# Linear-attention numerator: one reciprocal per sign, the division by the common denominator on GpSimd, and a longer lag of the output projection

## The chip, the cores and the metric

The kernel runs on one core of a Trainium2 chip. The metric is device microseconds (us) of one execution; a time given for a kernel is the median of several. In the profile the engines are PE (TensorE, matmuls), PEld (its weight loads), DVE (VectorE), ACT (ScalarE), POOL (GpSimd) and SP (SyncE, which here issues nearly all DMAs). A difference of about 0.5% is the least that a measurement of this kernel can tell from no change.

## The reference, cut to what matters

Two branches, A (linear attention) and B (an expert that runs for one token), are mixed by a gate per token. Only A is touched here.

```python
def _A_ref(x, wqkv, w_phi, wo):                       # S = 2048, D = 1024, H = 32 heads, Dh = 32
    q, k, v = split(x @ wqkv)
    pq, pk = per_head(q, w_phi), per_head(k, w_phi)
    phi_q = concat([softmax(pq), softmax(-pq)])       # two signs, 32 features each
    phi_k = concat([softmax(pk), softmax(-pk)])
    kv = einsum("bhsf,bhsd->bhfd", phi_k, v)
    z  = einsum("bhsf->bhf", phi_k)
    num = einsum("bhqf,bhfd->bhqd", phi_q, kv)
    den = einsum("bhqf,bhf->bhq", phi_q, z) + 1e-6
    return (num / den) @ wo

g = sigmoid((x * gate_w).sum(-1))
out = g * A + (1 - g) * B                             # B = x, plus one row from the expert
```

Written per head and token, with E+ = exp(pq) and E- = exp(-pq): sign s has a softmax sum S_s, a raw numerator N_s = E_s @ kv_s and a raw denominator D_s = E_s @ z_s. The wanted value is (N+/S+ + N-/S-) / (D+/S+ + D-/S-).

## The kernel before, in words

A first part makes x transposed (`xT`), the v projection, the folded weights `wkf` and `wqf` (w_phi multiplied into wk and wq) and the gates. A second part walks over keys and sums kv and z in PSUM. `kv_finish` (L431 to L452) copies them into `KV`. The third part, the one changed here, goes over queries; in the profile its first unit starts at 173.04 us.

- `q_front(sb, j)` (L458 to L467): for a block of 512 tokens and 128 features, 8 matmuls `pq` (L464) and two exps on ACT into `E` (L466, L467). There are 32 calls.
- `q_num(t, hf)` (L469 to L504): a *unit*. 32 units = 16 tiles `t` of 128 tokens x two halves `hf` of the heads. 8 matmuls `num` (L485), 4 per sign; each gives 128 numerator columns and 8 more (128 to 135) with each head's denominator and softmax sum. Then on DVE: `ds` (L489), `pr` (L491), `den` (L493), `rden` (L495), two halves of `ab` (L497, L498), and the large product `T` (L500, 128x1024 out of PSUM). GpSimd adds the two signs of `T` into `o_sb` (L504).
- `q_oT(t)` (L506 to L520): when both halves of a tile are there, a DMA transpose `oT` (L512) issued by SP; for the last tile 8 PE transposes into PSUM (`oT_ps`, L516) and a copy on ACT (L517). ACT also makes `xg`, the tile's share of x (L519).
- `q_wo(t, nh)` (L522 to L532): half an output tile: 8 matmuls `po` (L528), the gate and the addition of `xg` on DVE (`o_out`, L530), the store by SP (L532).

`num` has one buffer (three PSUM banks; pool `psK`, `bufs=1`): the matmuls of a unit wait until `T` of the unit before has read it. `po` and `oT_ps` share a ring of two PSUM banks (pool `psB`), handed out in the order of the code.

The loop at L596 to L612 sets the order: in step i unit n = i - 4, the transpose of the unit before it, front i, and one waiting `q_wo`. Units come in groups of eight (first halves of four tiles, then their second halves), so tiles become whole in units 4 to 7 of each group. A tile's two `q_wo` join the queue with a due step:

```python
wq_ += [(i + WL - 1, t, 0), (i + WL - 1, t, 1)]      # L605, WL = 4
```

In every other step, as long as there are any, 32 narrow matmuls of the expert (L374) come in as well. On every engine the instructions stand in a fixed order, made when the program is built from this loop and from what is ready when; the matmuls of one call can be split around those of another.

Of the kernel before, what the change touches and what calls it, by code (L numbers as in the profile page):

```python
# [8 lines left out]
BF = mybir.dt.bfloat16  # L9
F32 = mybir.dt.float32  # L10
I32 = mybir.dt.int32
U32 = mybir.dt.uint32
ALU = mybir.AluOpType
ACTF = mybir.ActivationFunctionType
AX = mybir.AxisListType
# [3 lines left out]
P = 128  # L19
S = 2048  # L20
D = 1024
H = 32
DH = 32
NT = S // P
KB = D // P
FF = 3584
NFB = FF // P
HH = 16
# [7 lines left out]
RANGE2 = 900.0  # L36
VC = [0, 352, 704, 1026]
VW = 1026


def general_path(tc, A_wqkv, A_w_phi, A_wo, x2, out2, gate, omg, y2, idx_pool, xT, wqf, ident, BDm):
# [116 lines left out]
def _bc(ap, shape):  # L158
    return ap.unsqueeze(len(shape) - 1).to_broadcast(shape)
# [3 lines left out]
def kernel(  # L163
# [4 lines left out]
    nc = tc.nc  # L168
# [10 lines left out]
    sm = main.enter_context(tc.tile_pool(name="sm", bufs=4))  # L179
# [34 lines left out]
    gate = const.tile([P, NT], F32, name="gate")  # L214
# [28 lines left out]
    def xload(t):  # L243
        xt_ = xs.tile([P, D], BF, name="xs_t", tag="xs")
        nc.sync.dma_start(out=xt_[:], in_=x2[t * P:(t + 1) * P, :])
        xtiles[t] = xt_

    wv_sb = wraw.tile([P, KB, VW], BF, name="wv_sb", tag="w16")
    xload(0)
# [6 lines left out]
    def rows_in():  # L256
        rows_ps = m2_ps[:, 0:KB].bitcast(BF)
        nc.tensor.transpose(out=rows_ps, in_=rows[:], identity=ident[0:2 * KB, 0:2 * KB])
        nc.vector.tensor_copy(out=wv_sb[:, :, D:VW].rearrange("p k c -> p c k"),
                              in_=rows_ps.rearrange("p (c k) -> p c k", c=2))  # L260
# [127 lines left out]
    def k_v(t, c):  # L388
# [7 lines left out]
        if c == 2:  # L396
            nc.vector.tensor_copy(out=rg[:, :, t], in_=pv[:, D - lo:VW - lo])

# [33 lines left out]
    def kv_finish():  # L432
        kvr = kvps[:, 0:16 * KSTR].rearrange("p (j half c) -> p j half c", half=2, c=KSTR)
        n = 0
        for half in range(2):
            for hh_ in range(2):
                h4 = half * 2 + hh_
                dst = slice(h4 * 32, h4 * 32 + 32)
                for sg in range(2):
                    q = hh_ * 2 + sg  # L440
                    src = slice(q * 32, q * 32 + 32)
                    zc = (128 + h4) if sg == 0 else (132 + h4)
                    sc = (132 + h4) if sg == 0 else (128 + h4)
                    kv_src = kvr[src, :, half, hh_ * 33:hh_ * 33 + DH]
                    z_src = kvr[src, :, half, hh_ * 33 + DH:hh_ * 33 + DH + 1]
                    if n % 2 == 0:
                        nc.vector.tensor_copy(out=KV[dst, sg, :, h4 * 32:h4 * 32 + 32], in_=kv_src)
                    else:
                        nc.scalar.copy(out=KV[dst, sg, :, h4 * 32:h4 * 32 + 32], in_=kv_src)
                    nc.vector.tensor_scalar_add(out=KV[dst, sg, :, zc:zc + 1], in0=z_src, scalar1=1e-6)  # L450
                    nc.gpsimd.memset(KV[dst, sg, :, sc:sc + 1], 1.0)
                    n += 1  # L452
# [16 lines left out]
    def q_num(t, hf):  # L469
        qw = qp["qw"]  # L470
        sb, tl = divmod(t, 4)
        E = est[sb]
        if hf == 0:
            st = {"o": qw.tile([P, H, DH], BF, name="o_sb", tag="o_sb", bufs=5)}
            xin = qw.tile([P, D], BF, name="xin", tag="xin", bufs=6)
            nc.sync.dma_start(out=xin[:], in_=x2[t * P:(t + 1) * P, :])
            st["xin"] = xin
            ost[t] = st
        st = ost[t]
        num = psK.tile([P, 3 * 512], F32, name="num", tag="kvn")  # L480
        for sg in range(2):
            for jl in range(4):
                b = sg * 4 + jl
                j = hf * 4 + jl
                nc.tensor.matmul(num[:, b * NSTR:b * NSTR + KVW], lhsT=E[:, j, sg, tl * P:(tl + 1) * P],  # L485
                                 rhs=KV[:, sg, j, :], start=True, stop=True)
        nb = num[:, 0:8 * NSTR].rearrange("p (b c) -> p b c", c=NSTR)
        ds = sm.tile([P, 4, 8], F32, name="ds", tag="ds")
        nc.vector.tensor_copy(out=ds[:], in_=nb[:, 4:8, 128:136])  # L489
        pr = sm.tile([P, 4, 8], F32, name="pr", tag="pr")  # L490
        nc.vector.tensor_tensor(out=pr[:], in0=nb[:, 0:4, 128:136], in1=ds[:], op=ALU.mult)  # L491
        den = sm.tile([P, 4, 4], F32, name="den", tag="den")
        nc.vector.tensor_tensor(out=den[:], in0=pr[:, :, 0:4], in1=pr[:, :, 4:8], op=ALU.add)  # L493
        rden = sm.tile([P, 4, 4], F32, name="rden", tag="rden")
        nc.vector.reciprocal(out=rden[:], in_=den[:])  # L495
        ab = sm.tile([P, 2, 4, 4], F32, name="ab", tag="ab")
        nc.vector.tensor_tensor(out=ab[:, 0, :, :], in0=nb[:, 4:8, 128:132], in1=rden[:], op=ALU.mult)  # L497
        nc.vector.tensor_tensor(out=ab[:, 1, :, :], in0=nb[:, 0:4, 132:136], in1=rden[:], op=ALU.mult)  # L498
        T = qw.tile([P, 2, HH, DH], F32, name="T", tag="T", bufs=2)
        nc.vector.tensor_tensor(  # L500
            out=T[:].rearrange("p s (j h) d -> p (s j) h d", h=4),
            in0=nb[:, :, 0:128].rearrange("p b (h d) -> p b h d", d=DH),
            in1=ab[:].rearrange("p s j h -> p (s j) h").unsqueeze(3).to_broadcast([P, 8, 4, DH]), op=ALU.mult)
        nc.gpsimd.tensor_tensor(out=st["o"][:, hf * HH:(hf + 1) * HH, :], in0=T[:, 0], in1=T[:, 1], op=ALU.add)  # L504

    def q_oT(t):  # L506
        qw = qp["qw"]
        st = ost[t]
        o_f = st["o"][:].rearrange("p h d -> p (h d)")
        oT = qw.tile([P, KB, P], BF, name="oT", tag="oT", bufs=3)  # L510
        if t < NT - 1:
            nc.sync.dma_start_transpose(out=oT[:], in_=o_f)  # L512
        else:
            oT_ps = psB.tile([P, KB, P], BF, name="oT_ps", tag="pB")
            for kb in range(KB):
                nc.tensor.transpose(out=oT_ps[:, kb, :], in_=o_f[:, kb * P:(kb + 1) * P], identity=ident[:])  # L516
            nc.scalar.copy(out=oT[:], in_=oT_ps[:])  # L517
        xg = qw.tile([P, D], F32, name="xg", tag="xg", bufs=2)
        nc.scalar.activation(out=xg[:], in_=st["xin"][:], func=ACTF.Copy, scale=omg[:, t:t + 1])  # L519
        st["oT"], st["xg"] = oT, xg  # L520

    def q_wo(t, nh):  # L522
        qw = qp["qw"]
        st = ost[t]
        sl = slice(nh * 512, (nh + 1) * 512)
        po = psB.tile([P, 512], F32, name="po", tag="pB")
        for kb in range(KB):
            nc.tensor.matmul(po[:], lhsT=st["oT"][:, kb, :], rhs=wo_sb[:, kb, sl], start=(kb == 0), stop=(kb == KB - 1))  # L528
        o_out = qw.tile([P, 512], BF, name="o_out", tag="o_out", bufs=4)
        nc.vector.scalar_tensor_tensor(out=o_out[:], in0=po[:], scalar=gate[:, t:t + 1],  # L530
                                       in1=st["xg"][:, sl], op0=ALU.mult, op1=ALU.add)
        nc.sync.dma_start(out=out2[t * P:(t + 1) * P, sl], in_=o_out[:])  # L532

    wq = [(0, kb) for kb in range(KB)] + [(1, kb) for kb in range(KB)]
# [38 lines left out]
    for i in range(NU + LAG):  # L573
# [9 lines left out]
        if i == 28:  # L583
            range_flag()
    qp["eb"] = None
    kv_finish()
    kscope.close()
    qp["eb"] = main.enter_context(tc.tile_pool(name="eb", bufs=2))
# [1 line left out]

    n_front = NSB * KB
    NL = 4
    WL = 4
    wq_ = []
    i = 0
    while i < n_front + NL + 2 or wq_:  # L596
        n = i - NL
        if 0 <= n < NU:
            sb, r = divmod(n, 8)
            q_num(sb * 4 + r % 4, r // 4)  # L600
        m = n - 1
        if 0 <= m < NU and m % 8 >= 4:
            t = (m // 8) * 4 + m % 4
            q_oT(t)
            wq_ += [(i + WL - 1, t, 0), (i + WL - 1, t, 1)]  # L605
        if i < n_front:
            q_front(i // KB, i % KB)
        if wq_ and (wq_[0][0] <= i):
            _, t, nh = wq_.pop(0)
            q_wo(t, nh)  # L610
        if i % 2 == 1 and ci < 21:
            ffn_chunk(ci)  # L612
            ci += 1
        i += 1
# [36 lines left out]
```

## Time and profile before

| | us |
|---|---|
| median of 3 runs (lowest, highest) | 319.48 (318.76, 319.93) |
| the profiled execution: its time | 317.62 |
| the profiled execution: its span, first to last instruction | 315.7 |
| PE busy in the span | 288.6 (91%) |
| DVE, ACT, POOL busy | 201.3, 144.0, 92.5 |
| mean granted TensorE clock | 0.981 of full speed |

The span is what the trace shows; the profiled execution's time is 1.92 us longer, and the median of the runs is 1.86 us above that. In rows of the timeline the columns are start, duration, engine, line, operation and tiles, how many were merged, and in brackets the engine's idle time before it and what ended that. A busy PE is not a PE at its peak; how densely it works is read from the starts of its matmuls.

### The profile page before, as it was taken

How to read it: one execution, taken by the hardware profiler on the slowest of the kernel's cores; microseconds unless marked ns; L12 is line 12 of the kernel's file. 1: busy time of each engine (PE TensorE's matmuls, PEld its weight loads, DVE VectorE, ACT ScalarE, POOL GpSimd, SP SyncE). 2: the span in 40 equal slices, each digit the busy share in tenths (PEclk: the TensorE clock that was granted, in tenths of full speed). 3: DMA queues.
4: the chain of work that ended last, by engine and by line, in shares of the span. 5: the costliest groups of instructions: out<-in, count | busy, mean ns of one | idle time of the engine just before them, and what ended most of it. 6: DMA issues, size and time to landing. Idle time of an engine off the chain costs nothing. (4 is left out here: it accounts for less than half of the span.)

```text
span 315.7 us, 6529 instructions
## 1 busy us (share of the span) xinstructions
PE 288.6 (91%) x2614; PEld 169.6 (54%) x2614; DVE 201.3 (64%) x438; ACT 144.0 (46%) x266; POOL 92.5 (29%) x73
## 2 busy tenths in 40 slices
PE   1999999999998999999979999999999999975790
PEld 1567777776544656656545565555555555532340
DVE  3201275753599977778793666877777777885540
ACT  3743378788754434444428544434444444220210
POOL 6000000000063567755550333333333333332301
PEclk9999999999999999999999999999999999996996
DMA  8999858610000798867737876522552256123221
GB/s 209 335 237 337 323 123 144 139 32 2 1 0 2 249 292 270 259 198 209 261 138 236 279 288 185 115 67 70 133 132 70 66 133 135 34 69 67 66 69 37
DMA packets 65585, 47.46 MB, mean 150 GB/s; under 512 B 35344, under 2 KB 56848, under 8 KB 65552
## 3 DMA queue, kind: packets, MB, share of 16 engines
q1 hardware_dynamic: 64400, 46.94, 52.4%
q8 instruction: 22, 0.36, 0.5%
q10 hardware_dynamic: 1120, 0.07, 0.2%
q14 instruction: 11, 0.09, 0.1%
q0 software_dynamic: 32, 0.00, 0.0%
HBM read 34.67 MB, written 4.20 MB: 123 GB/s over the span
## 5 line engine op out<-in xcount | busy, mean ns | idle before, releaser
L418 POOL TENSOR_TENSOR phi<-e,rs 128x1024 bf16<-128x1024 bf16 x24 | 45.7, 1912 | 111.1 <-DVE rs L415 98.9
L504 POOL TENSOR_TENSOR o_sb<-T 128x512 bf16<-128x512 f32 x32 | 40.6, 1267 | 93.8 <-DVE T L500 91.1
L528 PE MATMUL po<-wo_sb,oT 128*128 128x512 bf16 x256 | 64.2, 387 | 4.0 <-DMA oT<-o_sb 4.0
L393 PE MATMUL pv<-wv_sb,xT 128*128 128x352 bf16 (+1 forms) x384 | 63.9, 315 | 0.7 <-ACT v_all L395 0.6
L406 PE MATMUL pk<-wkf,xT 128*128 128x512 bf16 x256 | 60.6, 379 | 1.0 <-ACT e L410 1.0
L464 PE MATMUL pq<-xT,wqf 128*128 128x512 bf16 x256 | 61.1, 379 | 0.3 <-ACT E L467 0.3
L393 PEld LDWEIGHTS <-xT 128*128 128x128 bf16 x384 | 36.7, 99 | 17.4 <-DVE xT L268 0.5
L413 DVE TENSOR_REDUCE ssum<-e 128x32 f32<-128x1024 bf16 x32 | 38.6, 1208 | 9.6 <-ACT e L410 9.5
L500 DVE TENSOR_TENSOR T<-num,ab 128x1024 f32<-128x1024 f32 x32 | 39.2, 1224 | 3.2
L528 PEld LDWEIGHTS <-oT 128*128 128x128 bf16 x256 | 24.5, 100 | 29.7 <-DMA oT<-o_sb 4.4
L466 ACT ACTIVATE E<-pq 128x512 bf16<-128x512 f32 x32 | 19.0, 592 | 45.1 <-PE pq L464 40.3
L464 PEld LDWEIGHTS <-wqf 128*128 128x128 bf16 x256 | 24.2, 98 | 26.4
L519 ACT ACTIVATE xg<-xin,omg 128x1024 f32<-128x1024 bf16 x16 | 18.4, 1148 | 42.0 <-DVE o_out L530 19.2
L409 ACT ACTIVATE e<-pk 128x512 bf16<-128x512 f32 x32 | 19.1, 597 | 39.9 <-PE pk L406 22.0
L406 PEld LDWEIGHTS <-xT 128*128 128x128 bf16 x256 | 22.9, 97 | 23.8 <-issue 1.1
L530 DVE SCALAR_TENSOR_TENSOR o_out<-po,gate,xg 128x512 bf16<-128x512 f32 x32 | 24.0, 749 | 8.4 <-PE po L528 5.3
L395 ACT CAST v_all<-pv 128x352 bf16<-128x352 f32 (+1 forms) x48 | 20.8, 438 | 15.5 <-PE pv L393 15.5
L485 PE MATMUL num<-KV,E 128*128 128x136 bf16 x256 | 21.7, 229 | 2.3 <-DVE T L500 2.0
L485 PEld LDWEIGHTS <-E 128*128 128x128 bf16 x256 | 17.4, 101 | 11.3 <-DVE T L500 8.8
L489 DVE COPY ds<-num 128x32 f32<-128x32 f32 x32 | 6.1, 192 | 25.4 <-PE num L485 25.3
L268 DVE COPY xT<-pT 128x1024 bf16<-128x1024 bf16 x16 | 10.9, 688 | 17.2 <-PE pT L267 16.6
L410 ACT ACTIVATE e<-pk 128x512 bf16<-128x512 f32 x32 | 18.9, 591 | 0.0
(96 smaller groups left out, 269.9 us busy)
## 6 DMA issues: line engine op xcount, KB each, us to landing
wch<-in_B_w_gate_dram SPq DMA_DIRECT2D x7, 1024.0 KB, 5.9
wch<-in_B_w_up_dram SPq DMA_DIRECT2D x7, 1024.0 KB, 5.6
wchd<-in_B_w_down_dram SPq DMA_DIRECT2D x7, 1024.0 KB, 5.7
xs_t<-in_A_x_dram SPq DMA_DIRECT2D x16, 256.0 KB, 4.5
xin<-in_A_x_dram SPq DMA_DIRECT2D x16, 256.0 KB, 2.9
out_dram<-o_out SPq DMA_DIRECT2D x32, 128.0 KB, 2.0
wo_sb<-in_A_wo_dram SPq DMA_DIRECT2D x1, 2048.0 KB, 13.2
wv_sb<-in_A_wqkv_dram SPq DMA_DIRECT2D x2, 704.0 KB, 5.1
```

What stands on the lines that cost most here:

```text
L393: nc.tensor.matmul(pv[:, 0:hi - lo], lhsT=xT[:, kb, t * P:(t + 1) * P], rhs=wv_sb[:, kb, lo:hi], start=(kb == 0), stop=(kb == KB - 1))
L395: nc.scalar.copy(out=v_all[:, t, h0:h1, 0:DH], in_=pv[:, 0:(h1 - h0) * DH].rearrange("p (h d) -> p h d", d=DH))
L406: nc.tensor.matmul(pkf, lhsT=xT[:, kb, t * P:(t + 1) * P], rhs=wkf[:, kb, hf * 512:(hf + 1) * 512], start=(kb == 0), stop=(kb == KB - 1))
L409: nc.scalar.activation(out=e[:, :, 0, :], in_=pk[:], func=ACTF.Exp)
L413: nc.vector.tensor_reduce(out=ssum[:], in_=e2, axis=AX.X, op=ALU.add)
L418: eng.tensor_tensor(out=phi[:].rearrange("p h s f -> p (h s) f"), in0=e2, in1=_bc(rs[:], [P, HH * 2, DH]), op=ALU.mult)
L464: nc.tensor.matmul(pq[:], lhsT=wqf[:, kb, j * P:(j + 1) * P], rhs=xT[:, kb, sb * SB:(sb + 1) * SB], start=(kb == 0), stop=(kb == KB - 1))
L485: nc.tensor.matmul(num[:, b * NSTR:b * NSTR + KVW], lhsT=E[:, j, sg, tl * P:(tl + 1) * P], rhs=KV[:, sg, j, :], start=True, stop=True)
L500: nc.vector.tensor_tensor(out=T[:].rearrange("p s (j h) d -> p (s j) h d", h=4), in0=nb[:, :, 0:128].rearrange("p b (h d) -> p b h d", d=D ...
L504: nc.gpsimd.tensor_tensor(out=st["o"][:, hf * HH:(hf + 1) * HH, :], in0=T[:, 0], in1=T[:, 1], op=ALU.add)
L528: nc.tensor.matmul(po[:], lhsT=st["oT"][:, kb, :], rhs=wo_sb[:, kb, sl], start=(kb == 0), stop=(kb == KB - 1))
L530: nc.vector.scalar_tensor_tensor(out=o_out[:], in0=po[:], scalar=gate[:, t:t + 1], in1=st["xg"][:, sl], op0=ALU.mult, op1=ALU.add)
```

## The change

Each sign's 1024 numerator values are scaled by the reciprocal of that sign's own softmax sum (`rS`, taken for both signs at once, straight from PSUM) and the denominators likewise (`wD`). `T` no longer needs the common denominator. That is formed after `T` (`den`, a reduction over the two signs, and its reciprocal `rden`), and GpSimd applies it in a second instruction: first the sum of the signs in f32 (`U`), then the product with `rden` into `o_sb`. In `kv_finish` the columns of denominator and softmax sum get the same places for both signs. The lag `WL` goes from 4 to 6 steps, and rings get deeper: `T` 2 to 3, `xin` 6 to 8, `oT` 3 to 6, `xg` 2 to 4; `U` is new with 2. `TDV = 0` makes `t >= TDV` hold always, so the other branch in `q_wo` issues nothing.

```diff
-                    zc = (128 + h4) if sg == 0 else (132 + h4)
-                    sc = (132 + h4) if sg == 0 else (128 + h4)
+                    zc = 128 + h4
+                    sc = 132 + h4
...
-            xin = qw.tile([P, D], BF, name="xin", tag="xin", bufs=6)
+            xin = qw.tile([P, D], BF, name="xin", tag="xin", bufs=8)
...
-        ds = sm.tile([P, 4, 8], F32, name="ds", tag="ds")
-        nc.vector.tensor_copy(out=ds[:], in_=nb[:, 4:8, 128:136])
-        pr = sm.tile([P, 4, 8], F32, name="pr", tag="pr")
-        nc.vector.tensor_tensor(out=pr[:], in0=nb[:, 0:4, 128:136], in1=ds[:], op=ALU.mult)
-        den = sm.tile([P, 4, 4], F32, name="den", tag="den")
-        nc.vector.tensor_tensor(out=den[:], in0=pr[:, :, 0:4], in1=pr[:, :, 4:8], op=ALU.add)
-        rden = sm.tile([P, 4, 4], F32, name="rden", tag="rden")
-        nc.vector.reciprocal(out=rden[:], in_=den[:])
-        ab = sm.tile([P, 2, 4, 4], F32, name="ab", tag="ab")
-        nc.vector.tensor_tensor(out=ab[:, 0, :, :], in0=nb[:, 4:8, 128:132], in1=rden[:], op=ALU.mult)
-        nc.vector.tensor_tensor(out=ab[:, 1, :, :], in0=nb[:, 0:4, 132:136], in1=rden[:], op=ALU.mult)
-        T = qw.tile([P, 2, HH, DH], F32, name="T", tag="T", bufs=2)
+        rS = sm.tile([P, 8, 4], F32, name="rS", tag="rS")
+        nc.vector.reciprocal(out=rS[:], in_=nb[:, :, 132:136])
+        wD = sm.tile([P, 8, 4], F32, name="wD", tag="wD")
+        nc.vector.tensor_tensor(out=wD[:], in0=nb[:, :, 128:132], in1=rS[:], op=ALU.mult)
+        T = qw.tile([P, 2, HH, DH], F32, name="T", tag="T", bufs=3)
         nc.vector.tensor_tensor(
             out=T[:].rearrange("p s (j h) d -> p (s j) h d", h=4),
             in0=nb[:, :, 0:128].rearrange("p b (h d) -> p b h d", d=DH),
-            in1=ab[:].rearrange("p s j h -> p (s j) h").unsqueeze(3).to_broadcast([P, 8, 4, DH]), op=ALU.mult)
-        nc.gpsimd.tensor_tensor(out=st["o"][:, hf * HH:(hf + 1) * HH, :], in0=T[:, 0], in1=T[:, 1], op=ALU.add)
+            in1=rS[:].unsqueeze(3).to_broadcast([P, 8, 4, DH]), op=ALU.mult)
+        den = sm.tile([P, 4, 4], F32, name="den", tag="den")
+        nc.vector.tensor_reduce(out=den[:], in_=wD[:].rearrange("p (s j) h -> p j h s", s=2), axis=AX.X, op=ALU.add)
+        rden = sm.tile([P, HH], F32, name="rden", tag="rden")
+        nc.vector.reciprocal(out=rden[:], in_=den[:].rearrange("p j h -> p (j h)"))
+        U = qw.tile([P, HH, DH], F32, name="U", tag="U", bufs=2)
+        nc.gpsimd.tensor_tensor(out=U[:], in0=T[:, 0], in1=T[:, 1], op=ALU.add)
+        nc.gpsimd.tensor_tensor(out=st["o"][:, hf * HH:(hf + 1) * HH, :], in0=U[:],
+                                in1=_bc(rden[:], [P, HH, DH]), op=ALU.mult)
...
-        oT = qw.tile([P, KB, P], BF, name="oT", tag="oT", bufs=3)
+        oT = qw.tile([P, KB, P], BF, name="oT", tag="oT", bufs=6)
...
-        xg = qw.tile([P, D], F32, name="xg", tag="xg", bufs=2)
+        xg = qw.tile([P, D], F32, name="xg", tag="xg", bufs=4)
...
-    WL = 4
+    WL = 6
```

In the built program the change moves instructions at the end of the query part. Units are numbered 0 to 31; below, unit 29 has its numerators in `num_4139` before and in `num_4086` after, unit 30 in `num_4178` and `num_4124`, unit 31 in `num_4217` and `num_4162`. `oT_4162` (before) and `oT_4108` (after) are the transposed tile 12, whole with unit 28. `...` marks rows left out, mostly further rows of the same eight.

PE before, from unit 29 to the last tile's transposes:

```order
L485 MATMUL num_4139<-KV_114,E_3730 128x136
...
L528 LDWEIGHTS oT_4162
L528 MATMUL po_4269<-wo_sb_111,oT_4162 128x512
L485 LDWEIGHTS E_3730
L485 MATMUL num_4178<-KV_114,E_3730 128x136
...
L485 MATMUL num_4217<-KV_114,E_3730 128x136
...
L528 MATMUL po_4281<-wo_sb_111,oT_4162 128x512
L516 LDWEIGHTS o_sb_4055
L516 MATMUL oT_ps_4257<-ident_91,o_sb_4055 128x128
```

PE after, the same place:

```order
L486 MATMUL num_4086<-KV_114,E_3685 128x136
...
L530 MATMUL po_4150<-wo_sb_111,oT_3829 128x512
...
L486 MATMUL num_4124<-KV_114,E_3685 128x136
...
L530 MATMUL po_4188<-wo_sb_111,oT_3829 128x512
...
L486 MATMUL num_4162<-KV_114,E_3685 128x136
...
L530 MATMUL po_4188<-wo_sb_111,oT_3829 128x512
...
L517 MATMUL oT_ps_4201<-ident_91,o_sb_4004 128x128
...
L530 MATMUL po_4213<-wo_sb_111,oT_3881 128x512
...
L517 MATMUL oT_ps_4201<-ident_91,o_sb_4004 128x128
```

Before, nothing stands between units 28 and 29 but four `po` matmuls, four transposes and the expert's small one, and one `po` on tile 12 stands ahead of unit 30. After, ten `po` matmuls of tiles 9 and 10 stand between any two of units 28 to 31, and two of tile 10 behind unit 31; tile 12 comes only behind the last tile's transposes.

DVE before, from unit 29's `T` to unit 30's:

```order
L500 TENSOR_TENSOR T_4159<-num_4139,ab_4156 128x1024
L489 COPY ds_4187<-num_4178 128x32
L491 TENSOR_TENSOR pr_4189<-num_4178,ds_4187 128x32
L493 TENSOR_TENSOR den_4191<-pr_4189 128x16
L495 RECIPROCAL rden_4193<-den_4191 128x16
L497 TENSOR_TENSOR ab_4195<-num_4178,rden_4193 128x16
L498 TENSOR_TENSOR ab_4195<-num_4178,rden_4193 128x16
L500 TENSOR_TENSOR T_4198<-num_4178,ab_4195 128x1024
```

DVE after, from unit 29's `T` to unit 30's:

```order
L494 TENSOR_TENSOR T_4099<-num_4086,rS_4095 128x1024
L499 TENSOR_REDUCE den_4101<-wD_4097 128x16
L533 SCALAR_TENSOR_TENSOR o_out_4121<-po_4112,gate_116,xg_3782 128x512
L501 RECIPROCAL rden_4103<-den_4101 128x16
L490 RECIPROCAL rS_4133<-num_4124 128x32
L492 TENSOR_TENSOR wD_4135<-num_4124,rS_4133 128x32
L494 TENSOR_TENSOR T_4137<-num_4124,rS_4133 128x1024
```

Between a unit's matmuls and its `T` stand two small instructions instead of six, but behind `T` now come the rest of its own chain and an `o_out` before the next unit's turn.

More of the change, by code (lines that the diff above doesn't have):

```diff
@@ L38 @@
 VW = 1026
+TDV = 0
 def general_path(tc, A_wqkv, A_w_phi, A_wo, x2, out2, gate, omg, y2, idx_pool, xT, wqf, ident, BDm):
@@ L517, in q_oT @@
             nc.scalar.copy(out=oT[:], in_=oT_ps[:])
-        xg = qw.tile([P, D], F32, name="xg", tag="xg", bufs=2)
+        st["oT"] = oT
+        xg = qw.tile([P, D], F32, name="xg", tag="xg", bufs=4)
         nc.scalar.activation(out=xg[:], in_=st["xin"][:], func=ACTF.Copy, scale=omg[:, t:t + 1])
-        st["oT"], st["xg"] = oT, xg
+        st["xg"] = xg
     def q_wo(t, nh):
@@ L529, in q_wo @@
         o_out = qw.tile([P, 512], BF, name="o_out", tag="o_out", bufs=4)
-        nc.vector.scalar_tensor_tensor(out=o_out[:], in0=po[:], scalar=gate[:, t:t + 1],
-                                       in1=st["xg"][:, sl], op0=ALU.mult, op1=ALU.add)
+        if t >= TDV:
+            nc.vector.scalar_tensor_tensor(out=o_out[:], in0=po[:], scalar=gate[:, t:t + 1],
+                                           in1=st["xg"][:, sl], op0=ALU.mult, op1=ALU.add)
+        else:
+            ga = qw.tile([P, 512], F32, name="ga", tag="ga", bufs=3)
+            nc.scalar.activation(out=ga[:], in_=po[:], func=ACTF.Copy, scale=gate[:, t:t + 1])
+            nc.gpsimd.tensor_tensor(out=o_out[:], in0=st["xg"][:, sl], in1=ga[:], op=ALU.add)
         nc.sync.dma_start(out=out2[t * P:(t + 1) * P, sl], in_=o_out[:])
```

## The prediction

> **What bounds the kernel now.** I read the page's slices first, then stretches of the query part (columns: stretch, its length, busy time of PE, PEld, DVE, ACT and POOL with counts, granted clock, DMA share, GB/s).
>
> ```profile
> PE   1999999999998999999979999999999999975790
> PEclk9999999999999999999999999999999999996996
> ...
> 170.00:200.00 30.00, 29.37 (x323) 17.12 (x321) 18.92 (x61) 15.21 (x28) 8.88 (x7) 1.00 0.73 245
> 260.00:275.00 15.00, 15.00 (x95) 7.70 (x93) 11.24 (x32) 5.71 (x9) 4.89 (x4) 1.00 0.40 85
> 275.00:285.00 10.00, 7.05 (x53) 3.90 (x51) 8.49 (x25) 2.49 (x3) 3.79 (x3) 1.00 0.19 62
> 285.00:295.00 10.00, 7.04 (x32) 3.67 (x32) 5.87 (x18) 0.00 (x0) 2.53 (x2) 0.66 0.32 61
> 295.00:305.00 10.00, 7.91 (x41) 3.65 (x40) 4.16 (x6) 3.25 (x3) 1.27 (x1) 1.00 0.29 83
> ```
>
> PE is full until 275 us and has holes behind it, where the clock falls too. That "full" means dense there, the timeline shows:
>
> ```profile
> 267.75 0.64 PE L485 MATMUL num<-KV,E 128*128 128x136 bf16 x8
> ...
> 271.67 0.64 PE L485 MATMUL num<-KV,E 128*128 128x136 bf16 x8
> ...
> 275.60 0.64 PE L485 MATMUL num<-KV,E 128*128 128x136 bf16 x8
> 276.07 3.62 PE L528 MATMUL po<-wo_sb,oT 128*128 128x512 bf16 x16
> 276.27 0.19 DVE L489 COPY ds<-num 128x32 f32<-128x32 f32 x1 [0.16 <-PE num L485]
> ...
> 278.15 1.23 DVE L500 TENSOR_TENSOR T<-num,ab 128x1024 f32<-128x1024 f32 x1
> ```
>
> A unit's eight `num` hold PE for 0.47 us (275.60 to 276.07). With 16 matmuls of width 512 at 0.22 each (below) that is 3.97, and the units start every 3.92 to 3.93. So in the steady part DVE's chain, though it ends just before the next unit, costs PE nothing, and shortening it gains nothing. What is to be gained lies in the tail:
>
> ```profile
> 281.18 0.22 PE L381 MATMUL small_ps<-ident,yT 128*8 128x128 bf16 x1
> ...
> 282.08 1.23 DVE L500 TENSOR_TENSOR T<-num,ab 128x1024 f32<-128x1024 f32 x1
> 283.36 0.65 PE L485 MATMUL num<-KV,E 128*128 128x136 bf16 x8 [1.96 <-DVE T L500]
> 283.39 1.26 POOL L504 TENSOR_TENSOR o_sb<-T 128x512 bf16<-128x512 f32 x1 [2.66 <-DVE T L500]
> 284.05 0.19 DVE L489 COPY ds<-num 128x32 f32<-128x32 f32 x1 [0.74 <-PE num L485]
> ...
> 284.68 4.50 SPq L512 DMA_TRANSPOSE oT<-o_sb  x2
> ...
> 285.36 1.22 DVE L500 TENSOR_TENSOR T<-num,ab 128x1024 f32<-128x1024 f32 x1
> ...
> 287.96 0.61 PE L528 MATMUL po<-wo_sb,oT 128*128 128x512 bf16 x1 [3.95 <-DMA oT<-o_sb]
> ...
> 297.34 0.40 PE L516 MATMUL oT_ps<-ident,o_sb 128*128 128x128 bf16 x4 [2.09 <-POOL o_sb L504]
> ...
> 297.58 10.52 PE L528 MATMUL po<-wo_sb,oT 128*128 128x512 bf16 x48
> 297.78 1.01 ACT L517 COPY oT<-oT_ps 128x1024 bf16<-128x1024 bf16 x1
> ```
>
> Three waits: for unit 28's `T`, for tile 12's transpose (issued 284.68), for the last tile's `o_sb`. The last 48 `po` give 10.52 / 48 = 0.219 us each. The clock, in slices of 1 us:
>
> ```profile
> 286.00:287.00 1.00, 0.00 (x0) 0.00 (x0) 0.58 (x1) 0.00 (x0) 0.34 (x1) 0.75 1.13 209
> ...
> 292.00:293.00 1.00, 1.00 (x9) 0.84 (x8) 0.49 (x2) 0.00 (x0) 0.87 (x1) 0.50 0.00 0
> 293.00:294.00 1.00, 1.00 (x7) 0.49 (x5) 0.83 (x4) 0.00 (x0) 0.40 (x1) 0.84 0.00 0
> ...
> 296.00:297.00 1.00, 0.00 (x0) 0.00 (x0) 0.60 (x1) 0.32 (x1) 0.98 (x1) 1.00 0.25 86
> ...
> 310.00:311.00 1.00, 0.00 (x0) 0.00 (x0) 0.00 (x0) 0.00 (x0) 0.00 (x0) 0.70 0.25 73
> ```
>
> It halved at 286.5 (a slice of 0.75) and came back at 293.3 (0.84).
>
> From 281.40 (the end of the expert's small transpose) PE had left 3 units (1.41), 64 `po` (14.02) and 4 transposes (297.34 to 297.58, 0.24): 15.67 us, so 297.07 if dense. It ended at 308.10. **The tail loses 11.03 us**: 8.0 in the three waits, 3 in the slow clock and smaller waits.
>
> **The change, part by part.**
>
> ```profile
> L500 DVE TENSOR_TENSOR T<-num,ab 128x1024 f32<-128x1024 f32 x32 | 39.2, 1224 | 3.2
> L530 DVE SCALAR_TENSOR_TENSOR o_out<-po,gate,xg 128x512 bf16<-128x512 f32 x32 | 24.0, 749 | 8.4 <-PE po L528 5.3 <-ACT oT L517 3.0
> L415 DVE RECIPROCAL rs<-ssum 128x32 f32<-128x32 f32 x32 | 10.9, 344 | 1.8
> L495 DVE RECIPROCAL rden<-den 128x16 f32<-128x16 f32 x32 | 8.1, 253 | 1.1
> L491 DVE TENSOR_TENSOR pr<-num,ds 128x32 f32<-128x32 f32 x32 | 6.1, 191 | 1.1
> L493 DVE TENSOR_TENSOR den<-pr 128x16 f32<-128x16 f32 x32 | 5.7, 177 | 1.1
> L418 POOL TENSOR_TENSOR phi<-e,rs 128x1024 bf16<-128x1024 bf16 x24 | 45.7, 1912 | 111.1 <-DVE rs L415 98.9 <-DVE cc L324 4.4 <-DVE bb L341 3.8
> L504 POOL TENSOR_TENSOR o_sb<-T 128x512 bf16<-128x512 f32 x32 | 40.6, 1267 | 93.8 <-DVE T L500 91.1 <-DMA out_dram<-o_out 2.7
> ```
>
> *DVE up to `T`.* Before: 284.05 to 286.58, 2.53 us. After: `rS` as L415 (0.344; from PSUM, which no row shows; I put it between 0.25, as L495, and 0.45), `wD` as L491 (0.191), `T` unchanged (1.224), two gaps of 0.04: 1.84. Each `num` buffer is free 0.69 earlier. *Behind `T`:* `den` (0.18, as L493), in the tail an `o_out` (0.749), `rden` (0.253) and three gaps: 1.30 us in which the next unit's chain cannot start. DVE's total falls a little; it has room in the steady part (11.24 of 15).
>
> *GpSimd.* `U` as L504, 1.267. The product, 128x512 f32 with a broadcast operand: half of L418 is 0.956, L504 is 1.267, all of L418 is 1.912. I take 1.267, the nearest in shape and type, and keep the ends. The pair is 2.53 us per unit against 3.92: hidden in the steady part, where the lag of six units and the deeper rings cover the later `o_sb`. Exposed only in the tail, for the last tile.
>
> *Head of the query part.* Two more units run before the first `po`. Such a unit is 1.75 + 0.47 and half of the expert's 32 matmuls (182.22 to 183.03, 0.81): 2.63 us.
>
> ```profile
> 182.22 0.94 PE L374 MATMUL small_ps<-hh,wchd 128*128 128x1 bf16 x32
> ...
> 183.03 1.24 PE L464 MATMUL pq<-xT,wqf 128*128 128x512 bf16 x5
> ```
>
> From one unit's start to the next the DVE loop needs 0.67 (275.60 to 276.27) + 1.84 + 0.05 (`T`'s end at 283.31 to 283.36) = 2.56. Units without the expert's matmuls give 2.44, so every other one waits 0.12: 0.6 us in ten units, against 0.63 lost in 170 to 200 now. I count it as nothing, within 0.6 either way. GpSimd's 2.53 fits under 2.63, with a third `T` buffer.
>
> *SP.* The transposes of tiles 12 to 14 now have 0.75 us stores of older halves between them and land long before their `po`; the two more `xin` loads ahead of the first transpose wait for the first two `xg`, which ACT makes ahead of the first unit's end; it has room for the two further early `xg` (15.21 busy of 30). Nothing.
>
> *Tail, replayed* with zero at the start of unit 28, PE and DVE in their new order. PE has ten `po` (2.19) between units. `T`(28): DVE first finishes an `o_out` (0.2 to 0.95), so 0.98 + 1.84 = 2.82 (DVE reads PSUM 0.20 behind PE's last issue, as 276.07 to 276.27); PE is there at 0.47 + 2.19 = 2.66, unit 29 starts at 2.87 (wait 0.21). `T`(29) = 2.82 + 1.30 + 1.84 = 5.96; unit 30 at 6.01 (wait 0.48). `T`(30) 9.10, unit 31 at 9.15 (wait 0.48); `T`(31) 12.24. After unit 31 two `po` to 10.06, then transposes of the last tile's first half (0.06 wait for a buffer). The next `po` needs the PSUM buffer that `o_out` behind `T`(31) gives back, 13.25: starts at 13.30, **2.96 us idle**. GpSimd, 0.08 behind `T` (283.31 to 283.39): `U` 12.32 to 13.59, product to 14.87; the second transposes at 14.92 (0.74 idle), four `po` to 16.02, then a wait for ACT's copy (0.44 + 1.01 behind 14.92) to 16.42 (0.40). 72 `po` are left: 15.77, end 32.19. Work in it: 4 x 0.47 + 112 x 0.219 + 0.44 = 26.85; idle 5.33.
>
> The same work in the old trace: zero lies 26.85 - 15.67 = 11.18 before 281.40, at 270.22. End: 302.4 against 308.1, **5.7 us gained**. What follows (last `o_out`, store, the expert's row) is unchanged.
>
> *The clock.* It halved 2.5 us after PE's last matmul (284.0 to 286.5), and again 2.3 us after the end (308.1 to 310.4), in both cases with some work shortly before. The idle 2.09 us before 297.34 did not do it. The new hole is 2.96, with 0.88 of work and another 0.74 behind: nearer to the two that did. I expect one slow stretch, shorter than the old 6.8 us, since what follows is dense: half speed for 0.8 to 2.8 us of work, 0.4 to 1.4 lost; I take 1.0. Two such stretches would cost 2.5 to 3.
>
> [...]
>
> Sum: 5.7 - 1.0 = 4.7 us. Against the profiled execution 317.62 gives 312.9; on the median, 1.86 higher, **314.8**. About 0.5% (1.6 us) is what a measurement of this kernel can tell from no change.
>
> **The rivals.**
> *The clock stays up:* 313.8. For it: the 2.09 hole; against: the two drops. 0.20.
> *The gain is taken back in the tail:* the new waits at `T` and at the `po` buffer are longer (`rS` slow out of PSUM, the product at 1.912 adds 0.64) and the clock stays low for two stretches (3 us): 5.7 - 3 - 1 = 1.7 or less, 317.8. For it: `o_out` in front of every chain; against: none of the rows is that long. 0.20, half of it under 0.5%.
> *GpSimd becomes the bound (slower):* the pair is on every unit. If the product takes more than 3.92 - 1.27 = 2.65 us, `T` runs out of buffers, `num` is held and PE waits in each of 21 steady units. At 3.0 us: 0.35 x 21 = 7.4, and about 5 in the head: 319.48 + 12.4 - 4.7 = 327. Against: L418 needs 1.87 ns per element, L504 2.47; this would be 5.9. 0.08.
>
> **How the numbers follow.** The forecast has 0.52. Faster: 0.52 + 0.20 + half of 0.20 = 0.82; same 0.10; slower 0.08. The range goes from the clock staying up with the product at 0.956 and `rS` at 0.25 (0.3 + 0.4 less, 313.1) to the second rival (317.8), each widened by 0.6, half the spread of the runs before (318.76 to 319.93): 312.5 to 318.4.
>
> **What would show it.** `num` in the steady part still every 3.92 us; DVE 1.84 from `rS` to the end of `T`; POOL near 81 us in L503 and L504; no PE wait on the transposed tile 12; one hole of about 3 us at a `po` behind unit 31, for `o_out`, with a slow clock behind it. Wrong if GpSimd's product is far from 1.27, if `num` waits on `T` in the steady part, or if the hole is elsewhere.

## The result, and the profile after

| | before | after |
|---|---|---|
| median of the runs, us | 319.24 (318.76 to 319.93, 4 runs) | 310.26 (310.08 to 310.60, 4 runs) |
| profiled execution: time, span | 317.62, 315.7 | 310.08, 308.4 |
| ratio of the runs, 95% interval | | 0.9718 (0.9697 to 0.9740) |

The change saves 9.0 us. The forecast was 4.7 us, 314.8, with a range that began at 312.5: the sign and the place were right, the size was not. One run of the experiments below, of the kernel with 32 added matmuls, took 350.66 us at a mean clock of 0.851 and is left out of that kernel's ratio.

Page of the changed kernel, first the slices, then stretches of the query part (columns as in the prediction):

```profile
PE   1899999999998989999998899999999999996990
PEclk9999999999999999999999999999999999999997
...
260.00:275.00 15.00, 15.00 (x94) 7.78 (x93) 11.29 (x26) 5.55 (x8) 8.73 (x8) 1.00 0.13 43
275.00:285.00 10.00, 7.31 (x51) 3.81 (x49) 7.03 (x18) 3.31 (x3) 7.49 (x7) 1.00 0.71 122
285.00:295.00 10.00, 10.00 (x48) 4.52 (x47) 4.16 (x6) 1.15 (x1) 0.00 (x0) 1.00 0.20 66
```

One short stretch with holes is left, between 279 and 285 us, and the clock stays up until PE is done. The tail in the timeline, from unit 27 on:

```profile
266.56 0.64 PE L486 MATMUL num<-KV,E 128*128 128x136 bf16 x8
...
270.49 0.64 PE L486 MATMUL num<-KV,E 128*128 128x136 bf16 x8
...
270.96 2.32 PE L530 MATMUL po<-wo_sb,oT 128*128 128x512 bf16 x10
271.35 0.35 DVE L490 RECIPROCAL rS<-num 128x32 f32<-128x32 f32 x1
...
271.74 0.19 DVE L492 TENSOR_TENSOR wD<-num,rS 128x32 f32<-128x32 f32 x1
271.84 1.22 DVE L494 TENSOR_TENSOR T<-num,rS 128x1024 f32<-128x1024 f32 x1
272.98 0.18 DVE L499 TENSOR_REDUCE den<-wD 128x16 f32<-128x32 f32 x1
273.07 0.74 DVE L533 SCALAR_TENSOR_TENSOR o_out<-po,gate,xg 128x512 bf16<-128x512 f32 x1
...
273.12 0.65 PE L486 MATMUL num<-KV,E 128*128 128x136 bf16 x8
...
273.73 0.24 DVE L501 RECIPROCAL rden<-den 128x16 f32<-128x16 f32 x1
273.89 0.30 DVE L490 RECIPROCAL rS<-num 128x32 f32<-128x32 f32 x1
...
275.76 0.64 PE L486 MATMUL num<-KV,E 128*128 128x136 bf16 x8
...
278.23 1.27 POOL L503 TENSOR_TENSOR U<-T 128x512 f32<-128x512 f32 x1 [0.20 <-DVE T L494]
278.39 0.64 PE L486 MATMUL num<-KV,E 128*128 128x136 bf16 x8
...
279.56 1.21 DVE L494 TENSOR_TENSOR T<-num,rS 128x1024 f32<-128x1024 f32 x1
279.57 1.05 POOL L504 TENSOR_TENSOR o_sb<-U,rden 128x512 bf16<-128x512 f32 x1
...
281.58 1.02 PE L530 MATMUL po<-wo_sb,oT 128*128 128x512 bf16 x4 [1.75 <-DVE o_out L533]
...
283.30 0.40 PE L517 MATMUL oT_ps<-ident,o_sb 128*128 128x128 bf16 x4 [0.70 <-POOL o_sb L504]
...
284.80 1.46 PE L530 MATMUL po<-wo_sb,oT 128*128 128x512 bf16 x6 [0.24 <-ACT oT L518]
...
285.66 14.84 PE L530 MATMUL po<-wo_sb,oT 128*128 128x512 bf16 x68
```

Unit 28 still starts 3.93 us after unit 27, as in the steady part. Units 28 to 31 start 2.63 to 2.64 us apart: that is 0.47 for `num` and ten `po`, so PE hardly waits for `T` there. Its only holes are 1.75, 0.70 and 0.24 us, the first at `po` for the buffer that `o_out` gives back, as foreseen. The last `po` ends at 300.50, against 308.10.

The groups of the new instructions (count, busy time, mean ns, idle before):

```profile
L503 POOL TENSOR_TENSOR U<-T 128x512 f32<-128x512 f32 x32 | 40.6, 1268 | 43.5 <-DVE T L494 26.5
L504 POOL TENSOR_TENSOR o_sb<-U,rden 128x512 bf16<-128x512 f32 x32 | 33.6, 1049 | 2.5
...
L490 DVE RECIPROCAL rS<-num 128x32 f32<-128x32 f32 x32 | 11.2, 350 | 7.5 <-PE num L486 7.5
L492 DVE TENSOR_TENSOR wD<-num,rS 128x32 f32<-128x32 f32 x32 | 6.1, 191 | 1.1
L499 DVE TENSOR_REDUCE den<-wD 128x16 f32<-128x32 f32 x32 | 5.7, 177 | 0.0
```

### The profile page after: what moved, and what is told of

Its sections match the earlier page's. It is cut to its first block, busy times and chain, and to the rows that moved or that the text cites. A ratio compares the mean times of both kernels' runs of the same rounds, so it can differ in the third digit from the quotient of the medians.

```text
span 308.4 us, 6488 instructions
## 1 busy us (share of the span) xinstructions
PE 285.2 (92%) x2614; PEld 168.2 (55%) x2614; DVE 193.0 (63%) x374; ACT 144.6 (47%) x266; POOL 126.0 (41%) x105
## 5 line engine op out<-in xcount | busy, mean ns | idle before, releaser
L394 PE MATMUL pv<-wv_sb,xT 128*128 128x352 bf16 (+1 forms) x384 | 63.2, 313 | 1.5 <-ACT v_all L396 1.4
L530 PE MATMUL po<-wo_sb,oT 128*128 128x512 bf16 x256 | 59.3, 379 | 2.0 <-DVE o_out L533 1.8
L503 POOL TENSOR_TENSOR U<-T 128x512 f32<-128x512 f32 x32 | 40.6, 1268 | 43.5 <-DVE T L494 26.5
L467 ACT ACTIVATE E<-pq 128x512 bf16<-128x512 f32 x32 | 19.1, 597 | 46.3 <-PE pq L465 41.5
L494 DVE TENSOR_TENSOR T<-num,rS 128x1024 f32<-128x1024 f32 x32 | 38.9, 1214 | 0.2 <-DMA xin<-in_A_x_dram 0.2
L410 ACT ACTIVATE e<-pk 128x512 bf16<-128x512 f32 x32 | 19.1, 597 | 40.1 <-PE pk L407 22.6
L465 PEld LDWEIGHTS <-wqf 128*128 128x128 bf16 x256 | 23.4, 98 | 21.5
L504 POOL TENSOR_TENSOR o_sb<-U,rden 128x512 bf16<-128x512 f32 x32 | 33.6, 1049 | 2.5
L486 PEld LDWEIGHTS <-E 128*128 128x128 bf16 x256 | 17.1, 98 | 9.8 <-DVE T L494 2.9
L486 PE MATMUL num<-KV,E 128*128 128x136 bf16 x256 | 20.8, 223 | 0.5 <-DVE KV L451 0.2
L468 ACT ACTIVATE E<-pq 128x512 bf16<-128x512 f32 x32 | 18.9, 592 | 0.0
```

The lines of the kernel that those rows point to most:

```text
L394: nc.tensor.matmul(pv[:, 0:hi - lo], lhsT=xT[:, kb, t * P:(t + 1) * P], rhs=wv_sb[:, kb, lo:hi], start=(kb == 0), stop=(kb == KB - 1))
L465: nc.tensor.matmul(pq[:], lhsT=wqf[:, kb, j * P:(j + 1) * P], rhs=xT[:, kb, sb * SB:(sb + 1) * SB], start=(kb == 0), stop=(kb == KB - 1))
L494: nc.vector.tensor_tensor(out=T[:].rearrange("p s (j h) d -> p (s j) h d", h=4), in0=nb[:, :, 0:128].rearrange("p b (h d) -> p b h d", d=D ...
L503: nc.gpsimd.tensor_tensor(out=U[:], in0=T[:, 0], in1=T[:, 1], op=ALU.add)
```

## The experiments

All were compared with the kernel before on the same chip: 318.77 us (median of 13 runs, 316.74 to 320.29) beside the first four, 318.18 (19 runs, 317.33 to 320.98) beside the others.

**The lag without the chain.** The kernel before, with

```diff
-    WL = 4
+    WL = 6
```

and the deeper `xin`, `oT` and `xg`.

> The kernel before with WL = 6 and the deeper rings of xin, oT and xg; the seven DVE instructions and the single GpSimd addition stay. Theory A (the short chain up to T and behind it carries the gain; the lag alone does little, because the old DVE loop of about 3.3 us, 3.9 with an o_out in it, is longer than PE's 2.2 to 2.6 between the last units): 317 to 319 us, PE still waits for T at each of the last units. Rival B (the lag carries the gain, since older po work fills the tail): 310 to 312 us.

317.82 us, ratio 0.9967 (0.9941 to 0.9993). Theory A holds: the lag alone gives about 1 us, less than the 0.5% that a measurement of this kernel can tell from no change. The timeline of its tail:

```profile
281.23 0.65 PE L485 MATMUL num<-KV,E 128*128 128x136 bf16 x8 [2.91 <-DVE T L500]
...
289.72 0.65 PE L485 MATMUL num<-KV,E 128*128 128x136 bf16 x8 [0.56 <-DVE T L500]
...
293.01 0.65 PE L485 MATMUL num<-KV,E 128*128 128x136 bf16 x8 [0.75 <-DVE T L500]
...
297.63 0.40 PE L516 MATMUL oT_ps<-ident,o_sb 128*128 128x128 bf16 x4 [2.08 <-POOL o_sb L504]
```

There are older `po` to be had, but PE still waits for `T` at three units, and 2.08 us for the last `o_sb`, as in the kernel before (2.09).

**The chain without the lag.** The changed kernel, with

```diff
-    WL = 6
+    WL = 4
```

> The changed kernel with WL = 4 again; rings stay deep. Theory A: PE's order in the tail is the same up to which tile the po belong to, tile 12's transpose is there in time, so 310.3 us within 0.6. Rival B (the lag carries the gain): tile 12's transpose is waited for again, 314 us or more.

310.75 us (310.33 to 311.31), ratio 0.9759 (0.9716 to 0.9803) against the changed kernel's 0.9718 (0.9697 to 0.9740). The intervals overlap; nearly the whole gain is the chain's. PE shows the same two main holes:

```profile
284.98 1.02 PE L530 MATMUL po<-wo_sb,oT 128*128 128x512 bf16 x4 [1.75 <-DVE o_out L533]
286.71 0.61 PE L517 MATMUL oT_ps<-ident,o_sb 128*128 128x128 bf16 x4 [0.70 <-POOL o_sb L504]
```

PE's order in the tail comes with the chain: built with the shorter chain, the program has ten `po` between the last units with either lag. The order and the faster loop of DVE are not separated by a run. By the rows of before the order alone would hardly have removed the wait, since unit 28's `T` ended 3.78 us after its unit's start (279.53 to 283.31), and ten `po` bring PE there after 2.66. In this profiled execution, though not in that of the changed kernel, the clock fell, and it fell during the second of the two holes. Slices of 1 us (the granted clock is the third number from the end):

```profile
286.00:287.00 1.00, 0.30 (x4) 0.30 (x4) 0.00 (x0) 0.16 (x1) 0.65 (x1) 0.62 0.98 230
287.00:288.00 1.00, 1.00 (x6) 0.45 (x5) 0.00 (x0) 0.65 (x1) 0.00 (x0) 0.50 0.06 14
288.00:289.00 1.00, 1.00 (x4) 0.42 (x3) 0.00 (x0) 0.37 (x1) 0.00 (x0) 0.50 0.00 0
289.00:290.00 1.00, 1.00 (x5) 0.35 (x3) 0.75 (x1) 0.00 (x0) 0.00 (x0) 0.67 0.00 0
```

By the shares of these slices the clock was halved from 286.24 to 289.66, 3.4 us. The execution's 311.31 is 0.9 to 1.0 above the two runs with a mean clock of 0.995 and 0.996.

**The `po` buffer.** The changed kernel, with

```diff
-            oT_ps = psB.tile([P, KB, P], BF, name="oT_ps", tag="pB")
+            oT_ps = psA.tile([P, KB, P], BF, name="oT_ps", tag="pA")
```

> The changed kernel, with the last tile's PE transposes in a buffer of the ring that pq used (free in the tail) in place of one of the two po buffers. Theory A: the 1.75 us wait of po for o_out goes down to about 0.25, the wait for the last o_sb grows from 0.7 to about 1.05, ACT's copy blocks nobody: 1.5 us less, 308.8 us. Rival (the hole is only moved to the last o_sb, which sets the end anyway): 310.3 us.

308.98 us (308.42 to 309.32), ratio 0.9707 (0.9664 to 0.9751). On one chip beside the lag of 4 it is 1.8 us less; against the changed kernel's 310.26, measured on another occasion, 1.3. By the ratios to the kernel before it is only about 0.4 us less than the changed kernel, and the intervals overlap, so the times alone do not show the gain. The traces do: the last `po` ends 28.1 us after the start of unit 28, 30.0 in the changed kernel. The hole at `po` is gone, and one remains:

```profile
283.88 0.40 PE L517 MATMUL oT_ps<-ident,o_sb 128*128 128x128 bf16 x4 [0.93 <-POOL o_sb L504]
```

**A longer hole, for the clock.** The changed kernel with, behind L504, for the last unit alone, the product issued twice more:

```diff
+        for _ in range(2 if (t == NT - 1 and hf == 1) else 0):
+            nc.gpsimd.tensor_tensor(out=st["o"][:, hf * HH:(hf + 1) * HH, :], in0=U[:],
+                                    in1=_bc(rden[:], [P, HH, DH]), op=ALU.mult)
```

> The changed kernel, with GpSimd's product of the last unit alone issued three times (2.1 us more before the last tile's second transposes). Holes of PE in the tail become about 1.75 and 2.1 to 2.8 us. If only the wait counts: 1.3 to 2.1 us longer, 311.6 to 312.4 us, clock 1.00 throughout. If two such holes near each other halve the clock, as the prediction took for 2.96 and 0.74: 0.4 to 1.4 us more, 312.6 to 313.8, and slices of 0.5 behind the holes.

312.73 us median, but the runs spread from 311.71 (mean clock 0.993) to 313.97 (0.988). The profiled one is the longest:

```profile
286.66 0.40 PE L520 MATMUL oT_ps<-ident,o_sb 128*128 128x128 bf16 x4 [2.31 <-POOL o_sb L507]
286.90 17.39 PE L533 MATMUL po<-wo_sb,oT 128*128 128x512 bf16 x71
...
287.00:288.00 1.00, 1.00 (x7) 0.40 (x4) 0.00 (x0) 0.90 (x1) 0.00 (x0) 0.90 0.02 8
...
291.00:292.00 1.00, 1.00 (x5) 0.43 (x4) 0.00 (x0) 0.65 (x1) 0.00 (x0) 0.90 0.39 131
```

With holes of 1.75 and 2.31 us the clock halved from 287.8 to 291.2, again 3.4 us. The 313.97, just above the range of the expectation's second outcome, has the wait and a slow stretch. The 311.71 fits the first, the wait alone, but only the longest run has a trace. Three of these four runs have a mean clock of 0.988 or less, and one of the eight of the changed kernel and of the lag of 4. That fits a slow stretch being more frequent with the longer hole; the runs are too few to show it.

**GpSimd's margin.** The changed kernel with the product issued twice in every unit (`range(1)` in place of the condition above), and three times (`range(2)`).

> The changed kernel with GpSimd's product issued twice in every unit (1.27 + 2 x 1.05 = 3.37 us of GpSimd per unit). Theory A (GpSimd is hidden under PE's 3.93 us per unit, only the last tile shows): about 1.05 us more from the last tile and up to 1 for the clock behind a longer hole, 311.3 to 312.3 us. Rival (GpSimd is already on the path): 32 x 1.05 = 34 us more, 344 us.

> The same with the product issued three times (1.27 + 3 x 1.05 = 4.42 us per unit, above PE's 3.93): GpSimd becomes the bound as the prediction's third rival has it. 21 steady units x 0.49 = 10 us, some 8 to 11 in the head, 2 at the end: 328 to 335 us, PE waiting at num for T and DVE at T for U.

Twice: 318.82 us (316.72 to 319.86), the whole gain gone, not the 1 to 2 us expected. In the steady part theory A is right, PE's `num` still start every 3.92 us:

```profile
231.17 0.64 PE L486 MATMUL num<-KV,E 128*128 128x136 bf16 x8
...
235.09 0.64 PE L486 MATMUL num<-KV,E 128*128 128x136 bf16 x8
...
239.02 0.64 PE L486 MATMUL num<-KV,E 128*128 128x136 bf16 x8
```

But units come every 2.7 us on average in the head and every 2.63 in the tail, where GpSimd now needs 3.48 for each and falls behind. It shows at both ends:

```profile
194.26 1.31 SPq L516 DMA_TRANSPOSE oT<-o_sb  x1
195.67 0.52 SPq L371 DMA_DIRECT2D wchd<-in_B_w_down_dram  x1
...
201.26 0.97 PE L375 MATMUL small_ps<-hh,wchd 128*128 128x1 bf16 x32 [1.96 <-DMA wchd<-in_B_w_down_dram]
...
291.03 0.61 PE L520 MATMUL oT_ps<-ident,o_sb 128*128 128x128 bf16 x4 [4.12 <-POOL o_sb L507]
```

At the head the first transpose waits in SP's queue for a late `o_sb`, the expert's last weights wait behind it, and PE waits for those; at the end PE waits 4.12 us for the last `o_sb`. The clock is lower in the stretches at or behind these waits (0.89 from 200 to 215 us, 0.78 from 285 to 295) and 1.00 in those just ahead (175 to 200, 275 to 285). Three times: 352.03 us (2 runs), where 328 to 335 was expected. The mechanism of the prediction's third rival holds, the price does not:

```profile
310.38 1.26 POOL L503 TENSOR_TENSOR U<-T 128x512 f32<-128x512 f32 x1
...
314.98 1.26 POOL L503 TENSOR_TENSOR U<-T 128x512 f32<-128x512 f32 x1
...
324.26 0.61 PE L520 MATMUL oT_ps<-ident,o_sb 128*128 128x128 bf16 x4 [11.58 <-POOL o_sb L507]
```

GpSimd sets the pace. It needs 4.60 us for each unit, in head and tail too, not the 4.42 that the four durations add up to (the gaps between them make the rest). PE then waits 11.58 us for the last `o_sb`.

**PE's own work in the old tail.** The kernel before, with 32 matmuls more that do no useful work:

```diff
+FILL = {28: 8, 29: 8, 30: 6, 31: 10}
...
+    def filler(n):
+        pf = psA.tile([P, SB], F32, name="pf", tag="pA")
+        for k in range(n):
+            nc.tensor.matmul(pf[:], lhsT=ident[:], rhs=xT[:, 0, 0:SB], start=True, stop=True)
...
             q_num(sb * 4 + r % 4, r // 4)
+            if n in FILL:
+                filler(FILL[n])
```

> The kernel before with 32 matmuls more (identity against xT, into a free PSUM buffer, 6.9 us of PE work whose result is not used) put behind units 28 to 31, to fill PE's holes in the tail. If the tail's time is set by the chain of DVE, GpSimd and the transposes, and the slow clock is a loss of its own: no longer than before, with a clock of 1.00, 315 to 318 us. If PE's own work sets the tail: 6.9 us longer, about 325.

317.19 us, ratio 0.9950 (0.9920 to 0.9980): 6.9 us more of PE work, and it is no longer (1 us shorter by the medians). Most runs have a mean clock of 0.992 to 0.996, against 0.971 to 0.985 for the kernel before beside them. So the old tail was not bound by PE's work. In the profiled run the clock stayed up in the tail (the page's slices have 9 tenths or more from 182.5 to 309.5 us, and 7 from 174.6 to 182.5 instead). That part of the old tail was the slow clock fits this, but how much cannot be read off, since the build also put the `po` in another order.

**The last unit on DVE.** The version with `oT_ps` in `psA`, and

```diff
-        nc.gpsimd.tensor_tensor(out=U[:], in0=T[:, 0], in1=T[:, 1], op=ALU.add)
-        nc.gpsimd.tensor_tensor(out=st["o"]...
+        eng = nc.vector if (t == NT - 1 and hf == 1) else nc.gpsimd
+        eng.tensor_tensor(out=U[:], in0=T[:, 0], in1=T[:, 1], op=ALU.add)
+        eng.tensor_tensor(out=st["o"]...
```

> The version with the last tile's transposes in pq's ring, and the sum and product of the very last unit on DVE in place of GpSimd (two instructions of some 0.6 us against 1.27 + 1.05). The last o_sb comes about 1 us earlier and PE has 17 po ahead of it, so no hole is left behind the last unit: 1.0 to 1.3 us less than 308.98, 307.8 us. Rival (ACT's copy or o_out sets the end there): no change, 309.

307.59 us (307.23 to 309.31), ratio 0.9686 (0.9648 to 0.9724). Behind the last unit no wait is named any more:

```profile
284.09 0.40 PE L518 MATMUL oT_ps<-ident,o_sb 128*128 128x128 bf16 x4
284.32 13.76 PE L531 MATMUL po<-wo_sb,oT 128*128 128x512 bf16 x63
```

It beats the kernel before. Against the changed kernel and the version with `oT_ps` in `psA` its ratio is the lowest, but the intervals overlap. Against the latter, measured on another chip, the medians differ by 1.4 us, of which the missing wait explains 0.93.

## Why the prediction was wrong

*Right:* the steady part is bound by PE and gained nothing (3.92 us per unit still); the gain lies in the tail; the wait for tile 12's transpose is gone; a hole comes behind unit 31, at `po`, for `o_out`; POOL is hidden. `rS` out of PSUM took 350 ns (0.344 taken), `wD` 191 (191), `den` 177 (180), `T` 1.22 us. L503 and L504 kept POOL busy for 74.2 us, not 81, since the product was shorter than taken. A store between the last transposes holds SP's queue for 0.53 us (276.89 and 279.39), not the 0.75 taken.

*Wrong, the size.* 314.8 against 310.26 is 4.5 us, in three terms:

1. **The replay of the tail, 1.9 us** (PE's end predicted at 302.4, measured at 300.50). The step that failed is DVE's loop of 1.84 + 1.30 = 3.14 us. Measured: 1.71 (271.35 to 273.06) and 0.83 (273.06 to 273.89), 2.54. I had put a gap of 0.04 us between any two DVE instructions. In these rows there is a gap where the second reads the first's result (`rS` to `wD`, 0.04; `ab` to `T` in the kernel before, 0.11). Where it does not, the second starts before the first ends: `T` 0.09 before the end of `wD`, `den` 0.08 before the end of `T`, `o_out` 0.09 before the end of `den`. The trace of before had it, in the same chain from 284.05 to 286.58 that the prediction added up:

```profile
285.00 0.17 DVE L497 TENSOR_TENSOR ab<-num,rden 128x16 f32<-128x16 f32 x1
285.09 0.16 DVE L498 TENSOR_TENSOR ab<-num,rden 128x16 f32<-128x16 f32 x1
```

   `ab`'s second half starts 0.08 before the first ends. At 3.14 the loop is longer than PE's 2.66 and every unit waits; at 2.54 it is shorter than PE's 2.63 and none does. The waits of 0.21, 0.48 and 0.48 fell away, `T`(31) ended (279.56 + 1.21) 10.28 us after the start of unit 28 and not 12.24, and the hole was 1.75, not 2.96.

   GpSimd's product, 1.049 and not 1.267 us, shortened the last chain by another 0.2. Its nearest row was half of L418 (0.956), the form with a broadcast operand, not L504. Against that, the start of unit 28 was 0.27 us later than replayed.

2. **The clock, 1.0 us.** I charged one slow stretch, with 0.8 to 2.8 us of work at half speed, which was my estimate and stands in no row; the profiled execution of after had none. The first rival (the clock stays up) was right for it, but its reason was not: the same two holes brought a stretch of 3.4 us in the profile of the lag of 4. The step that failed is the one I shared with that rival, that the length of a hole decides; the last section has what the traces show of it.

3. **From the profiled execution to the median, 1.7 us.** I carried 1.86 us over from before; after, the median is 0.18 us above the profiled time. That difference is no constant of the machine. The kernel before spreads from 316.74 us (mean clock 0.984) to 320.29 (0.975) over 13 runs; the changed kernel's four runs spread by 0.52. The profile shown of before was one of its shorter executions. Part of what differs goes with the mean clock: the four runs at 0.975 took 319.26 to 320.29 us, the three at 0.984 and 0.985 took 316.74 to 318.59. But two runs at the same clock (0.984) also differ by 1.85 us, and that remainder is not explained.

What remains of the 4.5 is -0.1: the time from the last `po` to the end of the span (7.9, 7.6 before) and what lies around the span (1.68, 1.92 before) nearly cancel.

*The third rival, GpSimd as bound,* needed a product of 2.65 us by my count, PE's steady 3.92 less 1.27. Measured, 1.05 more per unit was enough to lose the whole gain, since head and tail give GpSimd 2.6 to 2.7 us, not 3.92. The changed kernel's own pair takes 2.4, so its margin in the tail is 0.2 us.

## What to carry to other kernels

A chain that is hidden in the steady part can still set the end: replay the tail unit by unit, with the pace that the units have there (2.63 us here, not 3.92), for every engine. When adding up a chain on DVE, look up in the trace how dependent and independent neighbours stand; 0.1 us per pair decided here whether PE waited at all. And where the clock falls in the holes of a tail in some executions and not in others, take the spread of many runs as part of the time that a gain in the tail can remove, and do not carry one profile's distance to the median over.

## What the runs showed of the hardware

By the clock of slices of 1 us, the slow stretch that came while PE had work left lasted 3.4 us in three traces: 286.24 to 289.66 (lag of 4), 287.8 to 291.2 (the last product three times) and 282.6 to 286.0 (the lag alone: a slice of 0.81, three of 0.50, one of 0.98). In the kernel before it lasted from 286.5 to 293.3, 6.8 us, twice that. There the clock fell again at 310.4, and the full-speed stretch between, 17.1 us, is five times 3.42. So the three changes of that one trace lie whole multiples of about 3.4 us apart; no run shows why.

In the 3.4 us ahead of its fall PE is busy for 42% with the lag of 4 (282.83 to 286.24, with the whole hole of 1.75 and the start of the next), for 33% with the longer hole (284.39 to 287.80) and for 19% in the kernel before (283.08 to 286.49). In the changed kernel 279.83 to 283.24 has the whole hole of 1.75 and most of the one of 0.70; PE is busy for 30% of it, and the clock stays at 1.00. So holes of the same length came with the slow clock in one execution and without it in another, and PE's share in such a stretch does not tell the two apart. Neither a limit for that share nor what else decides is shown by a run.
